# FFN1 of the last batch by seven half-width products per two tiles of d_ff, and batches 2 to 7 written out operation by operation

## The chip, the cores and the metric

The kernel runs on one core of one Trainium2 chip. The metric is the device time of one execution in microseconds, lower is better. Beside the times there is a profile of one execution: every instruction with its engine, start, duration and what it waited for. The engines are TensorE (PE, with its weight loads listed apart as PEld), VectorE (DVE), ScalarE (ACT), GpSimd (POOL, here an issuer of loads) and SyncE (SP, here an issuer of stores and transposes).

## The reference

Eight batches, twelve heads, 448 tokens, 64 values per head: attention with a squared ReLU in place of a softmax, then a feed-forward pair with a leaky ReLU whose slope differs by column.

```python
batch, n_heads, seq, head_dim = (8, 12, 448, 64)
scores = scale * np.matmul(q, k.transpose(0, 1, 3, 2))
attn = np.maximum(scores, 0.0) ** 2 / S
attn_out = np.matmul(attn, v)
x = attn_out.transpose(0, 2, 1, 3).reshape(B * S, H * D)        # 3584 x 768
h = x @ w_in                                                    # 768 x 2048
g = np.maximum(h, 0.0) + alpha * np.minimum(h, 0.0)
out = g @ w_out                                                 # 2048 x 768
```

## The kernel before, in words

**Attention.** Four heads of a batch form a quad; a batch has 3 quads, and there are 24. A quad's scores come in 7 chunks. A chunk (`c` in the plan) is four 64x64 matmuls of 448 columns into two PSUM banks (`score_mm`, L209). One ReLU empties both banks, on ACT (L218) or on DVE (L220), and a square follows in SBUF (`s`; DVE L231 or ACT L229). When the 7 squares of a quad are there, `v` runs 28 matmuls of 64x64 (L241) and two copies write the quad's part of `xT` (L253 on ACT, L255 on DVE). q and k reach the layout T through a copy into `perm` (L195) and a transposing DMA on SP's queue (L197); POOL touches the tile that landed (L418) and then issues the next loads.

**FFN1.** For each batch `xT` holds 6 slices of 128 by 448. A tile of d_ff (`f`, 16 per batch) is 6 full-array matmuls of 448 columns into one bank (L275). ACT makes `neg` = relu(-h) from the bank (L281), and DVE writes g = h + (1 - alpha) * neg as bf16 into `gT` (L282, one SCALAR_TENSOR_TENSOR). `gT` holds two batches: batch b may be written once every reader of batch b - 2 is through.

**FFN2.** Four tiles of 128 tokens are done plainly (`f2`, L300). The other 24 form 12 pairs. A pair is a 2x2 block product done in Winograd's form with 7 products of 8 matmuls each, 384 columns wide (L335), and not with 8 such products. Its sums S are made on DVE (L331), the sums of the weights `w_mix` once (L313), and the results are combined by ACT copies (L351, L356) and DVE additions (L340).

**Order.** The program is scheduled by hand. A plan is a string of words, and each word issues one or several instructions in that order on their engines; every engine takes its own in order and waits on semaphores for the others. Words of before are compound: `f` is the 6 matmuls, the ReLU and the DVE operation, `cADA` is three chunks with their ReLUs. One plan serves batches 3, 4 and 6 alike (`EACH`), the others have their own. PSUM has 8 banks; a word takes the bank that was taken longest ago (`one`, `take_pair`), so the words' order fixes the banks too. Batch 7 (`LAST`) runs its 16 `f`, then the last two FFN2 pairs. Its last product is cut in two (`p4e`, 256 and 128 columns), and its stores go alternately through SP and ACT from the word `z` on.

Of the kernel before, what the change touches and what calls it, by code (L numbers as in the profile page):

```python
# [20 lines left out]
def kernel(  # L21
# [50 lines left out]
    paired, two_queues = [], []  # L72
# [161 lines left out]
    def attnv(n, eng="AD"):  # L234
        ps = take_pair()
        vv = vraw.pop(n)
        for j in range(NJ):
            a = att.pop((n, j))
            for r in range(2):
                for s in range(2):  # L240
# [7 lines left out]
        if eng == "A":
            nc.scalar.activation(xT[b][:, g], ps[:, :, :S], ACTF.Copy, scale=out_scale)
            return  # L250
        for r in range(2):
            if eng[r] == "A":
                nc.scalar.activation(xT[b][:, g, r], ps[:, r, :S], ACTF.Copy, scale=out_scale)  # L253
            else:
                nc.vector.tensor_scalar(xT[b][:, g, r], ps[:, r, :S], out_scale, None, ALU.mult)  # L255
# [15 lines left out]
    gT = singles.tile([128, KF, 2 * S], BF16, name="gT")  # L271

    def f1_mm(ps, b, ff, ks):
        for km in ks:
            nc.tensor.matmul(ps, w_in_sb[:, km // 2, km % 2, bass.ts(ff, 128)],  # L275
# [3 lines left out]
    def f1_out(ps, b, ff):  # L279
        neg = neg_pool.tile([128, S], F32, tag="neg", name="neg")  # L280
        nc.scalar.activation(neg, ps, ACTF.Relu, scale=-1.0)  # L281
# [11 lines left out]
    def f2(sb, c, h, parts=None):  # L293

        first_col, width = COLS[h][0], COLS[h][1] - COLS[h][0]
        o = o_pool.tile([128, d_model - CUT], F32, tag="o", name="osb")
        for lo, hi in parts or ((0, width),):
            ps = take_bank()[:, :hi - lo]
            for ff in range(KF):
                nc.tensor.matmul(ps, gT[:, ff, bass.ts(c, 128)], w_out_sb[:, ff, first_col + lo:first_col + hi],  # L300
                                 start=(ff == 0), stop=(ff == KF - 1))
            nc.scalar.copy(o[:, lo:hi], ps)
            store(sb, c, first_col + lo, first_col + hi, o[:, lo:hi])
# [11 lines left out]
    class Pair:  # L315

        def __init__(self, a, b):
            self.a, self.b = a, b
            ga, gb = gT[:, :, bass.ts(a[1], 128)], gT[:, :, bass.ts(b[1], 128)]
            self.a11, self.a12, self.a21, self.a22 = ga[:, :KH], ga[:, KH:], gb[:, :KH], gb[:, KH:]  # L320
            self.s = {}

        def mix(self, *which):
            for i in which:
                t = self.s[2] if i == 4 else S_pool.tile([128, KH, 128], BF16, tag="S", name="S")
# [7 lines left out]
        def mm(self, ps, left, right, start):  # L333
            for i in range(KH):
                nc.tensor.matmul(ps, left[:, i], right[:, i], start=(start and i == 0), stop=(i == KH - 1),  # L335
                                 skip_group_check=not start)

        def plus(self, ps, u, keep=None):
            t = keep if keep is not None else o_pool.tile([128, d_model - CUT], F32, tag="o", name="osb")[:, :u.shape[-1]]
            nc.vector.tensor_tensor(t, ps, u, ALU.add)  # L340
            return t

        def kept(self, tag="u"):
            return u_pool.tile([128, NH], F32, tag=tag, name=tag)

        def p1(self):
            self.xb = hold()
            self.x = psum[:, self.xb, :NH]
            self.mm(self.x, self.a11, w_out_sb[:, :KH, :NH], True)
            self.m1 = self.kept("m")  # L350
            nc.scalar.copy(self.m1, self.x)  # L351

        def p2(self):
            self.mm(self.x, self.a12, w_out_sb[:, KH:, :NH], False)
            t = o_pool.tile([128, d_model - CUT], F32, tag="o", name="osb")[:, :NH]
            nc.scalar.copy(t, self.x)  # L356
            take(self.xb, 1)
            store(*self.a, 0, NH, t)
# [193 lines left out]
```

## Time and profile before

| | us |
|---|---|
| median of 3 runs | 373.29 (373.25, 373.29, 375.82) |
| span of the profiled execution, first to last instruction | 371.3 |
| TensorE with a matmul in it | 363.6 (98%) |
| VectorE busy | 278.0 (75%) |
| ScalarE busy | 274.7 (74%) |
| GpSimd busy | 71.7 (19%) |
| first matmul of batch 2's FFN1 | 109.18 |
| last matmul ends | 367.57 |

The page gives the span of the profiled execution and no time of its own beside it; the median of the runs lies 2.0 us above that span. Matmuls overlap in the array, so a matmul's recorded duration is longer than the distance to the next one; what a stream costs is the distance between starts. DVE and ACT records overlap in the same way by about a tenth of a microsecond. The granted TensorE clock is 1.00 in every stretch of the span.

### The profile page before, as it was taken

The numbers are of one execution on the slowest core, as the hardware profiler recorded it, in microseconds if no ns is written. First come the engines' busy times: TensorE is split into PE (matmuls) and PEld (weight loads), VectorE is DVE, ScalarE is ACT, GpSimd is POOL, SyncE is SP. The second block draws the span as 40 slices with busy tenths as digits, with TensorE's granted clock in tenths as the row PEclk, the third lists the DMA queues.
The fourth block names the chain that finished last, engine by engine and source line by source line (L and its number), as shares of the span: only waits on it lengthen the run. The fifth ranks groups of instructions, "written<-read, shape, count | busy, mean of one in ns | idle before, by whom it ended". The sixth has DMA issues, their size and how long they took to land.

```text
span 371.3 us, 7894 instructions
## 1 busy us (share of the span) xinstructions
PE 363.6 (98%) x3105; PEld 197.5 (53%) x3105; DVE 278.0 (75%) x445; ACT 274.7 (74%) x406; POOL 71.7 (19%) x120
## 2 busy tenths in 40 slices
PE   8799999999999999999999999999999999999995
PEld 6454564444554565545555455554555455555563
DVE  3989988885968989566887768888749667856653
ACT  5998676877997678885997859967699866964400
POOL 8566150304211222022020220202200000000000
PEclk9999999999999999999999999999999999999999
DMA  9999989999999868455882659727646201220024
GB/s 143 188 203 202 199 135 191 153 160 167 180 171 150 123 96 163 92 89 90 160 144 64 99 80 168 144 56 121 111 89 134 49 2 43 65 65 0 0 64 108
DMA packets 73557, 43.29 MB, mean 117 GB/s; under 512 B 40368, under 2 KB 73008, under 8 KB 73520
## 3 DMA queue, kind: packets, MB, share of 16 engines
q0 software_dynamic: 27136, 22.58, 42.0%
q1 hardware_dynamic: 45712, 19.61, 25.9%
q10 hardware_dynamic: 672, 0.59, 0.5%
q8 instruction: 24, 0.39, 0.4%
q14 instruction: 13, 0.11, 0.1%
HBM read 45.62 MB, written 11.01 MB: 153 GB/s over the span
## 4 chain that ended last, share of the span: by engine, by line
PE 94%; DVE 2%; ACT 2%; issue 1%; ACTq 0%
PE psum L275 38%; PE psum L335 30%; PE psum L241 9%; PE psum L209 9%; PE psum L300 6%; PE psum L183 1%; PE psum L165 1%; DVE gT L282 1%; ACT rl L218 1%; ACT xT L253 1%; ACT neg L281 1%; DVE w_mix L195 1%; DVE T L186 0%; DVE at L231 0%; DVE osb L340 0%
## 5 line engine op out<-in xcount | busy, mean ns | idle before, releaser
L275 PE MATMUL psum<-xT,w_in_sb 128*128 128x448 bf16 x768 | 150.4, 353 | 0.2 <-DVE gT L282 0.2
L282 DVE SCALAR_TENSOR_TENSOR gT<-neg,beta_sb,psum 128x448 bf16<-128x448 f32 x128 | 85.3, 679 | 43.4 <-ACT neg L281 42.1
L218 ACT ACTIVATE rl<-psum 128x896 bf16<-128x896 f32 x128 | 111.2, 925 | 6.7 <-PE psum L209 4.7
L275 PEld LDWEIGHTS <-w_in_sb 128*128 128x128 bf16 x768 | 73.4, 98 | 73.0 <-issue 6.8
L281 ACT ACTIVATE neg<-psum 128x448 f32<-128x448 f32 x128 | 68.5, 547 | 41.0 <-PE psum L275 32.7
L231 DVE TENSOR_TENSOR at<-rl 128x896 bf16<-128x896 bf16 x105 | 62.2, 620 | 0.5 <-ACT rl L218 0.2
L229 ACT ACTIVATE at<-rl 128x896 bf16<-128x896 bf16 x63 | 58.6, 952 | 0.3
L335 PEld LDWEIGHTS <-S 128*128 128x128 bf16 x384 | 36.7, 98 | 28.4 <-issue 5.3
L335 PE MATMUL psum<-w_mix,S 128*128 128x384 bf16 x288 | 49.8, 326 | 0.2
L220 DVE TENSOR_SCALAR rl<-psum 128x896 bf16<-128x896 f32 x40 | 43.2, 1086 | 8.7 <-PE psum L209 8.1
L209 PE MATMUL psum<-T 64*64 64x448 bf16 x672 | 45.9, 357 | 2.0 <-DVE T L186 1.0
L418 POOL COPY landed<-T 1x1 bf16<-1x1 bf16 x18 | 3.3, 181 | 206.1 <-DMA T<-perm 182.9
L335 PEld LDWEIGHTS <-gT 128*128 128x128 bf16 x296 | 28.3, 98 | 20.2 <-issue 1.8
L241 PE MATMUL psum<-at,vraw 64*64 64x448 bf16 x672 | 36.6, 350 | 0.0
L335 PE MATMUL psum<-w_out_sb,gT 128*128 128x384 bf16 x192 | 34.0, 326 | 0.0
L340 DVE TENSOR_TENSOR osb<-psum,u 128x384 f32<-128x384 f32 (+2 forms) x37 | 20.2, 547 | 12.6 <-PE psum L335 8.2
L209 PEld LDWEIGHTS <-T 64*64 64x64 bf16 x672 | 17.4, 105 | 22.7 <-issue 14.8
L241 PEld LDWEIGHTS <-vraw 64*64 64x64 bf16 x672 | 21.2, 106 | 11.9 <-issue 2.9
L300 PE MATMUL psum<-w_out_sb,gT 128*128 128x256 bf16 (+1 forms) x128 | 22.0, 326 | 0.1
L255 DVE TENSOR_SCALAR xT<-psum 128x448 bf16<-128x448 f32 x24 | 14.9, 622 | 8.9 <-PE psum L241 8.3
L253 ACT ACTIVATE xT<-psum 128x448 bf16<-128x448 f32 x24 | 13.3, 556 | 9.1 <-PE psum L241 8.7
L356 ACT COPY osb<-psum 128x384 f32<-128x384 f32 x12 | 5.8, 480 | 17.4 <-PE psum L335 17.4
(45 smaller groups left out, 242.0 us busy)
## 6 DMA issues: line engine op xcount, KB each, us to landing
out_dram<-osb SPq DMA_DIRECT2D x91, 96.0 KB, 2.2
vraw<-in_v_dram POOLq DMA_DIRECT2D x24, 224.0 KB, 6.5
qraw<-in_q_dram POOLq DMA_DIRECT2D x23, 224.0 KB, 4.1
kraw<-in_k_dram POOLq DMA_DIRECT2D x23, 224.0 KB, 5.3
w_in_sb<-in_moe_w_in_dram POOLq DMA_DIRECT2D x16, 192.0 KB, 8.0
w_out_sb<-in_moe_w_out_dram POOLq DMA_DIRECT2D x4, 512.0 KB, 9.5
w_out_sb<-in_moe_w_out_dram POOLq DMA_DIRECT2D x4, 256.0 KB, 8.8
out_dram<-osb SPq DMA_DIRECT2D x8, 128.0 KB, 3.2
```

The lines of the kernel that those rows point to most:

```text
L209: nc.tensor.matmul(ps[64 * c:64 * c + 64, r, :S], t[64 * r:64 * r + 64, 1, j, 64 * c:64 * c + 64], t[64 * r:64 * r + 64, 0, :, 64 * c:64 * ...
L218: nc.scalar.activation(rl, ps[:, :, :S], ACTF.Relu)
L220: nc.vector.tensor_scalar(rl, ps[:, :, :S], 0.0, None, ALU.max)
L229: nc.scalar.activation(a, rl, ACTF.Square)
L231: nc.vector.tensor_tensor(a, rl, rl, ALU.mult)
L241: nc.tensor.matmul(ps[64 * s:64 * s + 64, r, :S], vv[64 * r:64 * r + 64, s, j, :], a[64 * r:64 * r + 64, s], start=(j == 0), stop=(j == NJ ...
L275: nc.tensor.matmul(ps, w_in_sb[:, km // 2, km % 2, bass.ts(ff, 128)], xT[b][:, km // 2, km % 2, :], start=(km == 0), stop=(km == KM - 1))
L281: nc.scalar.activation(neg, ps, ACTF.Relu, scale=-1.0)
L282: nc.vector.scalar_tensor_tensor(gT[:, ff, (b % 2) * S:(b % 2) * S + S], neg, beta_sb[:, ff:ff + 1], ps, ALU.mult, ALU.add)
L300: nc.tensor.matmul(ps, gT[:, ff, bass.ts(c, 128)], w_out_sb[:, ff, first_col + lo:first_col + hi], start=(ff == 0), stop=(ff == KF - 1))
L335: nc.tensor.matmul(ps, left[:, i], right[:, i], start=(start and i == 0), stop=(i == KH - 1), skip_group_check=not start)
L340: nc.vector.tensor_tensor(t, ps, u, ALU.add)
```

## The change

Up to and including batch 1 the instructions are the same. Behind that two things differ.

**FFN1 of batch 7.** Its 16 tiles of d_ff are taken two at a time, in 8 `Quad`s. Two tiles of d_ff by 448 tokens by 768 is a 2x2 block product: weights in four quarters of 3 x 128 by 128, tokens in four quarters of 3 x 128 by 224. It is done by 7 products of 3 matmuls with 224 columns, in place of 2 x 6 matmuls with 448 columns (the same work as 8 products). The sums of the weights (`W`, `w_in_mix`) and of the tokens (`T`, `tok_mix`) are made on DVE; they lie in buffers of the raw, v, perm and at pools, and the third weight sum replaces a quarter of `w_in_sb`. A quad owns two PSUM banks, x and y. Its products run in the order 1, 2/5, 6, 7, 3, 4 with steps between them on ACT (small letters s, u, w) or DVE (capitals): s copies 224 columns from bank x to bank y, u and w copy 224 columns from y to SBUF, v and z add 224 columns (DVE, from PSUM and SBUF into PSUM). n is one ACT ReLU over both banks (896 columns), g and h are the two SCALAR_TENSOR_TENSOR that write `gT`.

**Order of batches 2 to 7.** One plan of 965 words replaces the six. A word is now one operation with its bank written out: `f6` the 6 matmuls into bank 6, `N6` the ReLU, `G6` the DVE operation, `c4` a chunk's matmuls into banks 4 and 5, `r4A` its ReLU on ACT, `+b63` product 6 of pair b into bank 3, `-b6` its output, `*ba` a sum. So operations of several words are interleaved as the string says, and more chunks stand early: 63 chunks by the word `+e42` against 50 up to the same amount of TensorE work before. `p4e` is gone; `z` stands two words before the last product.

```diff
-        if not paired:
-            return order[0]
-        mate = max(free, key=lambda i: taken[i]) ^ 1
-        return mate if mate in order[:4] and taken[mate] < 10**9 else order[0]
+        return free[0]
...
+    def w_in_mix(i, p, count, home):
+        a11, a12, a21, a22 = w_in_quarters(p, count)
...
+        x, y, op = {1: (a21, a22, ALU.add), 2: (made(1), a11, ALU.subtract),
+                    3: (a11, a21, ALU.subtract), 4: (a12, made(2), ALU.subtract)}[i]
+        nc.vector.tensor_tensor(t, x, y, op)
...
+    def tok_mix(i):
...
+        x, y, op = {1: (b12, b11, ALU.subtract), 2: (b22, tok_sum.get(1), ALU.subtract),
+                    3: (b22, b12, ALU.subtract), 4: (b21, tok_sum.get(2), ALU.subtract)}[i]
+        nc.vector.tensor_tensor(t, x, y, op)
...
+        def mm(self, ps, left, right, start):
+            for k in range(KI):
+                nc.tensor.matmul(ps, left[:, k], right[:, k], start=(start and k == 0), stop=(k == KI - 1),
+                                 skip_group_check=not start)
...
+            if c == "1":
+                self.mm(x[:, :HS], a11, b11, True)
+            elif c == "2":
+                self.mm(x[:, :HS], a12, b21, False)
+            elif c == "3":
+                self.mm(x[:, HS:S], self.w(4), b22, False)
+            elif c == "4":
+                self.mm(y[:, :HS], a22, tok_sum[4], False)
+            elif c == "5":
+                self.mm(x[:, HS:S], self.w(1), tok_sum[1], False)
+            elif c == "6":
+                self.mm(y[:, :HS], self.w(2), tok_sum[2], False)
+            elif c == "7":
+                self.mm(y[:, :HS], self.w(3), tok_sum[3], False)
+            elif c in "sS":
+                (nc.scalar.copy if c == "s" else nc.vector.tensor_copy)(y[:, :HS], x[:, :HS])
+            elif c in "uU":
+                (nc.scalar.copy if c == "u" else nc.vector.tensor_copy)(u[:, :HS], y[:, :HS])
+            elif c in "wW":
+                (nc.scalar.copy if c == "w" else nc.vector.tensor_copy)(u[:, HS:], y[:, :HS])
+            elif c == "v":
+                nc.vector.tensor_tensor(y[:, HS:S], x[:, HS:S], u[:, HS:], ALU.add)
+            elif c == "z":
+                nc.vector.tensor_tensor(x[:, HS:S], x[:, HS:S], u[:, :HS], ALU.add)
+            elif c == "n":
...
+                nc.scalar.activation(self.neg, psum[:, self.lo:self.lo + 2, :S], ACTF.Relu, scale=-1.0)
+            elif c in "gh":
...
+                nc.vector.scalar_tensor_tensor(gT[:, ff, (NB % 2) * S:(NB % 2) * S + S], self.neg[:, i],
+                                               beta_sb[:, ff:ff + 1], psum[:, self.lo + i, :S], ALU.mult, ALU.add)
...
-    LAST = """B f s0A f f f f s3A s2A s2A f f s2A f f f f f f pc f f s0A f p1 r1 pa pb p2 p6 p7 pd ra p5 rb rc p4 p3 r6 z r7 rd r5 r2 r3 r4e"""
...
+    P[4] = """*ba f0 f1 sA kqD kkA *bb f2 sD sA N0 +b63 N2 sD sD *bc f4 G0 N1 G2 N4 -b6 f5 c6 c2 G1 c0 G4 sA f4 r6D N5 f6 sD t r2A kqD r0A f7 N4 c2 kkA G5 G4 N6 r2A
```

The rows below show what stands on two engines at the places that the prediction speaks of. First VectorE at the start of batch 2, before; gT rows are FFN1's operations, at rows squares, rl rows ReLUs, S rows the sums of an FFN2 pair.

```order
97 L220 TENSOR_SCALAR rl<-psum 128x896
98 L282 SCALAR_TENSOR_TENSOR gT<-neg,beta_sb,psum 128x448 x2
99 L231 TENSOR_TENSOR at<-rl 128x896 x3
100 L282 SCALAR_TENSOR_TENSOR gT<-neg,beta_sb,psum 128x448 x2
101 L231 TENSOR_TENSOR at<-rl 128x896
102 L282 SCALAR_TENSOR_TENSOR gT<-neg,beta_sb,psum 128x448 x4
```

VectorE at the same place after the change:

```order
97 L217 TENSOR_SCALAR rl<-psum 128x896
98 L415 TENSOR_TENSOR S<-gT 128x1024
99 L693 COPY perm<-qraw 128x896
100 L415 TENSOR_TENSOR S<-S,gT 128x1024
101 L228 TENSOR_TENSOR at<-rl 128x896 x3
102 L415 TENSOR_TENSOR S<-gT 128x1024
103 L659 SCALAR_TENSOR_TENSOR gT<-neg,beta_sb,psum 128x448 x2
104 L396 TENSOR_TENSOR u<-psum,m 128x384
105 L659 SCALAR_TENSOR_TENSOR gT<-neg,beta_sb,psum 128x448 x2
106 L217 TENSOR_SCALAR rl<-psum 128x896
```

The sums of the second FFN2 pair, one copy into `perm` and a pair's output have moved ahead of batch 2's first FFN1 operations, which now stand behind seven other operations and not behind one.

Second, VectorE in FFN1 of batch 7 and behind it, before:

```order
279 L282 SCALAR_TENSOR_TENSOR gT<-neg,beta_sb,psum 128x448 x13
280 L331 TENSOR_TENSOR S<-gT 128x1024
281 L282 SCALAR_TENSOR_TENSOR gT<-neg,beta_sb,psum 128x448 x3
282 L331 TENSOR_TENSOR S<-gT 128x1024
283 L331 TENSOR_TENSOR S<-S,gT 128x1024
```

VectorE in a piece of FFN1 of batch 7 after the change; L525, L527 and L529 are s, u and w of a quad, L531 is v, L533 is z, L541 is g or h, L464 a sum of weights, L415 and L396 belong to FFN2 pairs:

```order
330 L533 TENSOR_TENSOR psum<-psum,uu 128x224
331 L396 TENSOR_TENSOR osb<-psum,u 128x384
332 L464 TENSOR_TENSOR w_in_sb<-w_in_sb 128x3x2x128
333 L533 TENSOR_TENSOR psum<-psum,uu 128x224
334 L541 SCALAR_TENSOR_TENSOR gT<-ng,beta_sb,psum 128x448
335 L525 COPY psum<-psum 128x224
336 L541 SCALAR_TENSOR_TENSOR gT<-ng,beta_sb,psum 128x448 x2
337 L415 TENSOR_TENSOR S<-S,gT 128x1024
338 L464 TENSOR_TENSOR w_in_sb<-w_in_sb 128x3x2x128
339 L525 COPY psum<-psum 128x224
340 L541 SCALAR_TENSOR_TENSOR gT<-ng,beta_sb,psum 128x448
```

Thirteen like operations in a row are replaced by operations of two or three quads in turn, with two FFN2 pairs (i and j of the plan) between them; before, those pairs stood ahead of batch 7's FFN1.

More of the change, by code (lines that the diff above doesn't have):

```diff
@@ L71 @@
     taken = [0] * 8
-    paired, two_queues = [], []
+    two_queues = []
     clock = [0]
@@ L189, in turn_dma @@
         if n in (5, 7, 8):
+            assert not mixed[2 + n % 2]
             w = w_mix[2 + n % 2].rearrange("p k c -> p (k c)")[:, :4 * NJ * D]
@@ L291, in store, with f2_mm, f2_out, f2 @@
             eng.dma_start(out=rows[j][:, lo:hi], in_=t[64 * u:64 * u + 64])
-    def f2(sb, c, h, parts=None):
-        first_col, width = COLS[h][0], COLS[h][1] - COLS[h][0]
-        o = o_pool.tile([128, d_model - CUT], F32, tag="o", name="osb")
[L297 to L303, printed above, removed]
+    def f2_mm(sb, c, h, i):
+        may_read((sb, c))
+        if (sb, c) in f2_half:
+            f2_done.add((sb, c))
+            has_read((sb, c))
+        f2_half.add((sb, c))
+        lo, hi = COLS[h]
+        for ff in range(KF):
+            nc.tensor.matmul(psum[:, i, :hi - lo], gT[:, ff, bass.ts(c, 128)], w_out_sb[:, ff, lo:hi],
+                             start=(ff == 0), stop=(ff == KF - 1))
+    def f2_out(sb, c, h, i):
+        lo, hi = COLS[h]
+        o = o_pool.tile([128, d_model - CUT], F32, tag="o", name="osb")
+        nc.scalar.copy(o[:, :hi - lo], psum[:, i, :hi - lo])
+        store(sb, c, lo, hi, o[:, :hi - lo])
+    def f2(sb, c, h):
+        i = one()
+        take(i, 1)
+        f2_mm(sb, c, h, i)
+        f2_out(sb, c, h, i)
+    mixed = [0] * 4
     def weight_mix(i, lo, hi):
+        assert not i or mixed[{1: 0, 2: 0, 3: 1}[i]] > mixed[i]
+        mixed[i] += 1
         b11, b12 = w_out_sb[:, lo:hi, :NH], w_out_sb[:, lo:hi, NH:]
@@ L331, in mix @@
                 nc.vector.tensor_tensor(t, x, y, op)
[L333 to L358, printed above, removed]
@@ L392, in p4y, with run @@
-        def p4y(self):
-            self.p4x(256, NH)
-        def p4e(self):
-            self.p4(((0, 256), (256, NH)))
-        def p3(self):
-            self.mm(self.z, self.s[4], w_out_sb[:, KH:, NH:], False)
-            store(*self.a, NH, d_model, self.plus(self.z, self.u2))
-            take(self.zb, 1)
+        def run(self, name):
+            if name in "23":
+                i = self.held.pop({"2": "1", "3": "5"}[name])
+                take(i, 1)
+            elif name in "15":
+                i = self.held[name] = hold()
+            else:
+                i = one()
+                take(i, 1)
+            self.product(name, psum[:, i, :NH])
+            self.output(name)
@@ new lines @@
+Q44 Q5u Q3h Q614 Q4z Q4n -j5 Q6S Q52 Q4g Q57 Q55 Q5w Q4h Q5v Q66 +j36 Q712 Q53 Q6u Q7S Q5z -j3 Q67 Q54 Q76 Q6w Q7U Q62 Q65 Q72 Q5n Q6v Q77 Q75 Q63 Q7w
+Q7v Q6z Q64 Q73 Q5g Q74 +j47 Q6n Q7z Q7n Q5h +k16 -k1A Q6g Q7g Q6h Q7h +l10 *lc +k26 +l71 *ka *kb *kc +k64 +k75 +k42 -l1D *kd *la -j4 -k6 *lb -k2A
++k53 +l64 -k7 -k5 -k4 +k33 *ld +l55 +l42 -k3 -l6 -l7 -l5 +l35 -l4 z -l3 +l20 -l2A"""
+    for i in range(4):
+        walk(P[i])
+    Line(walk)(P[4])
+    assert all(p.done == 7 for p in walk.pairs)
+    assert not stream and not late and turn["v"] == NQ and f2_done == {(0, 0), (0, 1), (0, 2), (2, 5)}
```

331 lines of the change are left out of this document (257 added, 74 removed).

## The prediction

> **What bounds the kernel now.** I read the page first: the share of each engine, and the chain that ended last.
>
> ```profile
> PE 363.6 (98%) x3105; PEld 197.5 (53%) x3105; DVE 278.0 (75%) x445; ACT 274.7 (74%) x406; POOL 71.7 (19%) x120
> PE 94%; DVE 2%; ACT 2%; issue 1%; ACTq 0%
> ```
>
> The chain is TensorE's. A busy 98% alone would not say so, because matmuls overlap. So I take the distance between starts from the timeline, at three widths: FFN1 (448 columns, the window opens after its first matmul), FFN2 products (384), and the last seven matmuls of the program (128). The fourth row is the weight loads of those narrow ones.
>
> ```profile
> 331.22 18.13 PE L275 MATMUL psum<-xT,w_in_sb 128*128 128x448 bf16 x95
> 349.19 4.06 PE L335 MATMUL psum<-w_out_sb,gT 128*128 128x384 bf16 x24
> 353.09 1.14 PE L335 MATMUL psum<-w_mix,S 128*128 128x384 bf16 x6
> 367.02 0.55 PE L335 MATMUL psum<-w_mix,gT 128*128 128x128 bf16 x7
> L335 PEld LDWEIGHTS <-gT 128*128 128x128 bf16 x8 | 0.5, 98 | 0.0
> L335 PE MATMUL psum<-w_mix,gT 128*128 128x128 bf16 x8 | 0.6, 219 | 0.0
> ```
>
> 95 matmuls of 448 columns take 349.19 - 331.22 = 17.97 us, 189.2 ns each. 24 of 384 take 353.09 - 349.19 = 3.90 us, 162.5 ns. Seven of 128 take 0.55 us; less the 0.219 of the last, six distances of 55 ns. The three lie on a line: 0.417 ns per column and 2.4 ns. So in FFN1 of batch 7 TensorE streams without a gap, and a change gains only by fewer columns or by waits elsewhere.
>
> How much waiting is there elsewhere? The chain gives a whole batch between two equal places:
>
> ```profile
> 152.57 9.19 PE psum L275 x48
> 198.52 9.19 PE psum L275 x48
> ```
>
> 45.95 us. It holds 96 matmuls of 448 (18.17 us), 14 products of 8 by 162.5 ns (18.20), 21 chunks and 3 words `v`, whose 64x64 matmuls run four at a time: 42 groups of one 448-column stream, 0.188 (7.90): 44.27 in all. The other 1.68 are turns between full-array and 64x64 matmuls, and waits. A turn is priced by this:
>
> ```profile
> 104.81 0.33 PE L335 MATMUL psum<-w_mix,gT 128*128 128x384 bf16 x1
> 105.06 0.76 PE L209 MATMUL psum<-T 64*64 64x448 bf16 x12
> 105.76 1.47 PE L335 MATMUL psum<-w_out_sb,S 128*128 128x384 bf16 x8
> 188.22 0.76 PE L209 MATMUL psum<-T 64*64 64x448 bf16 x12
> 189.04 2.27 PE L335 MATMUL psum<-w_mix,S 128*128 128x384 bf16 x13
> ```
>
> Three chunks (0.564) take 0.70 at 105.06, so 0.14 to turn back. The full-array matmul at 104.81 streams until 104.97, and the chunk starts at 105.06, 0.09 later: about 0.22 for a pair of turns. At 188.22 the same work takes 0.82: there TensorE waits 0.12. With 6 pairs of turns the batch has 1.32, and 0.36 of waits is left, of which about 0.25 are such visible ones. Over batches 2 to 6 that is 5 x 0.25, some **1.2 us that a better order can win**, and no more.
>
> **The change part by part.** The order of the built program gives the counts. FFN1 of batch 7: 96 matmuls of 448 go, 8 x 7 x 3 = 168 of 224 come. On the line, 224 columns cost 0.417 x 224 + 2.4 = 95.8 ns. 96 x 0.1892 = 18.16 against 168 x 0.0958 = 16.10: **-2.07 us**, on the path.
>
> The weight loads are the question here: 98 ns each, more than 95.8. But the 128-column matmuls above have a load each of 98 ns and follow at 55 ns, so loads overlap and do not set the pace. The Trainium skill says otherwise on its page TensorE: Matmul & The Clock Gate, section Back-to-back issue gap: with a weight load per matmul it gives about 81 ns for 128 columns, and under LDWEIGHTS columns / 1.2, which is 107 ns for 128. At 107 ns the 168 would take 18.0 us, an estimate by that page, and the sum below would end 1.9 us later. The row of 55 ns speaks against both figures, so I count nothing for it.
>
> Turns: the order has 34 stretches of 64x64 matmuls from batch 2 on, 28 before. 6 x 0.22 = **+1.3 us**, on the path.
>
> The old waits of 1.2 us go, where the new order covers them. What new ones come depends on DVE and ACT:
>
> ```profile
> 109.20:225.80 116.60, 116.48 (x927) 62.22 (x924) 88.53 (x142) 91.72 (x138) 21.68 (x37) 1.00 0.69 115
> 331.00:371.30 40.30, 36.57 (x220) 20.80 (x216) 21.97 (x36) 11.16 (x21) 0.00 (x0) 1.00 0.18 46
> 112.97 1.69 DVE L231 TENSOR_TENSOR at<-rl 128x896 bf16<-128x896 bf16 x3
> 114.58 1.27 DVE L282 SCALAR_TENSOR_TENSOR gT<-neg,beta_sb,psum 128x448 bf16<-128x448 f32 x2
> L282 DVE SCALAR_TENSOR_TENSOR gT<-neg,beta_sb,psum 128x448 bf16<-128x448 f32 x48 | 32.0, 679 | 19.5 <-ACT neg L281 19.3
> L220 DVE TENSOR_SCALAR rl<-psum 128x896 bf16<-128x896 f32 x40 | 43.2, 1086 | 8.7 <-PE psum L209 8.1 <-issue 0.4
> L331 DVE TENSOR_TENSOR S<-gT 128x1024 bf16<-128x1024 bf16 x24 | 15.9, 685 | 0.0
> L313 DVE TENSOR_TENSOR w_mix<-w_out_sb 128x1536 bf16<-128x1536 bf16 x4 | 3.7, 952 | 0.0
> L229 ACT ACTIVATE at<-rl 128x896 bf16<-128x896 bf16 x63 | 58.6, 952 | 0.3
> L253 ACT ACTIVATE xT<-psum 128x448 bf16<-128x448 f32 x24 | 13.3, 556 | 9.1 <-PE psum L241 8.7
> ```
>
> In a row of windows the numbers behind the stretch are its length, then PE, PEld, DVE, ACT. Back to back an operation costs 0.09 less than its record: three squares 1.69 = 2 x 0.535 + 0.62, two gT operations 1.27 = 0.59 + 0.68. The first 469 words of the new order hold, by the spacings above, as much TensorE work as the stretch 109.2 to 225.8. In them DVE has 11 more ReLUs (1.00 each), 11 squares (0.53) and 7 copies into perm (about 0.53, as a square of the same shape), less 2 sums, 2 outputs and an xT copy (2.7): 88.5 + 11.0 + 5.8 + 3.7 - 2.7 = **106.3 of 116.6**, 91%. ACT gains 6 squares (0.95), 5 xT copies (0.56) and 2 ReLUs and loses a perm copy and 4 outputs: about +7, 99 of 116.6. So both still fit, with 10 us of slack on DVE.
>
> I followed the order by hand with these costs, a matmul's result 0.2 after its stream. At the start of batch 2 the two engines stand at
>
> ```profile
> 109.18 7.17 PE L275 MATMUL psum<-xT,w_in_sb 128*128 128x448 bf16 x37
> 109.56 1.08 DVE L220 TENSOR_SCALAR rl<-psum 128x896 bf16<-128x896 f32 x1
> ```
>
> From 109.56 DVE has a ReLU, three sums, a copy, three squares, gT of banks 0 and 2, an output and gT of bank 1: 1.0 + 1.8 + 0.53 + 1.6 + 1.2 + 0.47 + 0.6 = 7.2, done at 116.8. TensorE by then has f0, f1, f2 (3.41), b63 (1.30), f4, f5 (2.27), two chunks and a turn (0.47) from 109.18, so it is at 116.63 and c0, which needs bank 1, waits 0.25. The next f4 waits as much for G4. From the start of batch 3's FFN1 I followed 60 us and found no wait: the banks come free 0.3 to 3 us early. In the last 75 us I found one of 0.14 (product 3 of the last quad, behind v). So 0.65 in 155 of 258 us; scaled to the whole **+1.1 us**.
>
> In the Quad part DVE has 16 additions (v, z), 8 copies, 4 token sums and 15 weight sums more. No row has an operation that writes PSUM from DVE or ACT. The nearest are reads of it:
>
> ```profile
> L340 DVE TENSOR_TENSOR osb<-psum,u 128x256 f32<-128x256 f32 x1 | 0.4, 425 | 0.3 <-PE psum L335 0.3
> L340 DVE TENSOR_TENSOR osb<-psum,u 128x128 f32<-128x128 f32 x1 | 0.3, 291 | 0.0
> L302 ACT COPY osb<-psum 128x256 f32<-128x256 f32 x4 | 1.5, 373 | 3.7 <-PE psum L300 3.7
> ```
>
> 224 columns on that line: 0.39 on DVE, and under 0.37 on ACT. The bounds are 0.29 (128 columns) and 0.68 (the gT operation on 448); I take 0.39, nearest in width. 24 x 0.30 back to back = 7.2 us; weight sums of 768 elements 0.55 (between 685 ns for 1024 and 952 for 1536, 0.52 per element), 14 x 0.46 + 0.87 = 7.3; token sums 4 x 0.42 = 1.7. Together 16 us, spread over the last 100 us, in which DVE had room (21.97 of 40.30 at the end): hidden, but for 10 us in the middle of the quads, where with these costs the order has 9.7 us of DVE to 10.1 of TensorE. If that cover goes, each 0.1 us per operation there costs about 1 us. ACT has spare time there. What hides a quad's chain of some 6.5 us (product, copy, product, copy ... ReLU, two gT operations) is the other quads and 14 FFN2 products of 1.30.
>
> The end: the last product is whole, so its copy on ACT reads 384 columns.
>
> ```profile
> 367.61 0.29 DVE osb L340
> L356 ACT COPY osb<-psum 128x384 f32<-128x384 f32 x12 | 5.8, 480 | 17.4 <-PE psum L335 17.4
> out_dram<-osb ACTq DMA_DIRECT2D x3, 96.0 KB, 2.4
> out_dram<-osb ACTq DMA_DIRECT2D x1, 32.0 KB, 1.9
> ```
>
> Copy +0.19, landing +0.5, less some 0.5 because the stores of the piece before no longer stand in the queues: **+0.1** (0 to 0.7).
>
> ```profile
> T<-perm SPq DMA_TRANSPOSE x16, 4.0
> ```
>
> Moved DMAs: the transposes and loads follow the perm copies. Each quad's copies stand at least 7 us of TensorE work ahead of its first chunk, against the 4.0 us from transpose to landing; the stores on SP's queue have no reader. Nothing counted.
>
> Sum: -2.07 + 1.3 - 1.2 + 1.1 + 0.1 = -0.8; span 371.3 - 0.8 = 370.5, and with the 2.0 us between span and the median of the runs **372.5 us**.
>
> **The rivals.** (1) The new waits do not come: -2.07 + 1.3 - 1.2 + 0.1 = -1.9, 371.4 us. For it: the stretch of 60 us without one. Against: the 0.25 above.
>
> (2) Operations that write PSUM cost more, 0.2 us each (towards the row of 448 columns). In the Quad part the cover on DVE is gone, 8 quads wait in turn for v and z: 16 x 0.2 = 3.2, of which I let 0.7 be hidden; 372.5 + 2.5 = 375.0 us. Nothing in the profile excludes it.
>
> (3) Slower: DVE becomes the bound from batch 2 to 4. Before, it stood idle 19.5 us ahead of its 48 gT operations in that stretch, waiting for ACT (row above). The new order leaves it 10.3. If it idles as before, 106.3 + 19.5 = 125.8 against 116.6, 9.2 us more than TensorE needs: 382 us. It decides from 10 us of such idling. Against it: other work of DVE now stands between the gT operations, so that the wait for ACT passes under it.
>
> **How the numbers follow.** Forecast 0.50, rival 1 0.20, rival 2 0.16, rival 3 0.14. What a measurement here can tell from no change is about 1%, 3.7 us. To gain that much, TensorE would have to save more than -2.07 and all waits together, 3.3 us without the turns: 0.03 for faster. Slower by over 1%, beyond 377.0: rival 3, 0.14. Same 0.83. The range runs from 371.0 (rival 1 with turns at 0.15) to 376.5 (rival 2 with 0.1 more an operation, or rival 3 with 14 us idle).
>
> **What would show it.** In the new profile: 224-column matmuls about 96 ns apart (the Quad line's 18 or so in the windows); 64x64 stretches 34; DVE busy near 106 in the first 117 us behind 109.2, and its idle time ahead of gT operations under 10; a v or z row near 0.39. Rival 2 would show as PE waiting for DVE L531 or L533, rival 3 as PE waiting for DVE's gT and rl operations in batches 2 to 4. I am wrong if the loads set the pace of the narrow matmuls, or if TensorE waits over 3 us in all from batch 2 on.

## The result, and the profile after

The changed kernel takes 379.23 us (median of 7 runs, 375.17 to 382.76), the kernel before 373.25 us (7 runs, 372.88 to 375.82). The ratio is 1.0121 with a 95% interval of 1.0085 to 1.0158: slower by somewhat over 1%. It leaves out the two runs of 381.04 and 382.76 us, which lie over 1.5% above the fastest run of the same kernel, and so is smaller than the quotient of the two medians, 1.016. The forecast was 372.5 us with a range up to 376.5, so it missed, and it missed on the side to which it had given 0.14. The runs of the changed kernel also spread over 7.6 us, those of the kernel before over 2.9.

The profiled execution took 379.88 us, its span 378.1. From its page, the busy time and shares of the engines, three rows of the 40 slices, and the chain that ended last, by engine and by line:

```profile
PE 363.5 (96%) x3166; PEld 202.0 (53%) x3169; DVE 303.2 (80%) x502; ACT 264.3 (70%) x399; POOL 72.3 (19%) x120
PE   8699999999999599999999999999999999999995
PEclk9999999999999699999999999999999999999999
DMA  9999989999999787978999853824123120021125
PE 85%; DMA 7%; DVE 4%; ACT 2%; issue 1%; POOL 1%; ACTq 0%; DVEq 0%; POOLq 0%; SPq 0%
PE psum L303 30%; PE psum L379 27%; PE psum L237 9%; PE psum L206 8%; PE psum L330 6%; DMA T<-perm 5%; PE psum L501 4%; DMA kraw<-in_k_dram 2%; DVE gT L311 1%; PE psum L175 1%; ACT neg L310 1%; DVE w_mix L188 1%; DVE rl L217 0%; DVE at L228 0%; ACT perm L188 0%
```

TensorE is as busy as before in sum (363.5 against 363.6 us) and the span is 6.8 us longer. The loss is in one place: the fourteenth of the 40 slices, about 123 to 132 us, shows TensorE at 5 tenths and its clock at 6. And a new name stands in the chain, `DMA T<-perm` with 5%: the DMA that transposes a quad's q and k out of the buffer `perm`.

The timeline of TensorE there (start, length, line, operation), and then the waits of all engines in 118 to 128 us (in all, times, longest):

```profile
121.51 0.57 PE L206 MATMUL psum<-T 64*64 64x448 bf16 x8
126.97 2.83 PE L237 MATMUL psum<-at,vraw 64*64 64x448 bf16 x28 [4.89 <-DVE gT L659]
```

```profile
POOL landed L435 <- DMA T<-perm: 11.4, 1, 11.4
DVE perm L693 <- DMA T<-perm: 5.5, 1, 5.5
PEld L237 <- issue: 5.1, 1, 5.1
PE psum L237 <- DVE gT L659: 4.9, 1, 4.9
ACT perm L693 <- DMA T<-perm: 4.8, 1, 4.8
```

TensorE has nothing to do for about 5 us, ahead of the product of scores and v that the plan calls v4 (word 49 of the plan, counted from 0). It waits for DVE's operation into gT, which frees banks 4 and 5. But DVE is not busy then: it stands for 5.5 us in front of a copy into `perm`, ACT for 4.8 us in front of another, and both wait for the transposing DMA. These are the copies of quad 12 (words 36 `kqD` and 41 `kkA`), which stand ahead of G5 and G4 in the queues, and `perm` has one buffer, which quad 11's DMA is still reading. The chain of waits, in order of time (start, length):

```profile
111.80 0.53 DVE perm L693
112.33 0.18 DVE S L415
112.50 12.52 DMA T<-perm
...
125.12 0.62 DVE perm L693
125.74 1.19 DVE gT L659 x2
...
126.97 2.83 PE psum L237 x28
```

Issued at 112.50, the transposition landed at 125.03, 12.5 us later, where the typical one before took 4.0. But 4.0 is a median of 16. In the kernel before the three transpositions issued at 102.5, 114.0 and 123.6 us took 6.8 to 7.0 us, and that of quad 11 is the second of them. The rows below show it, first before and then after. GpSimd issues four loads at this place, the last two in the `vraw` rows. Before, the transposition goes out 1.9 us behind the last of them, at 114.03; in the changed kernel it goes out between the two, at 112.50. The `landed` row is GpSimd's one-element copy right behind a landing.

```profile
111.40 1.44 POOL L124 DMA_DIRECT2D vraw<-in_v_dram  x2
114.03 12.73 SPq L197 DMA_TRANSPOSE T<-perm  x2
121.17 0.18 POOL L418 COPY landed<-T 1x1 bf16<-1x1 bf16 x1 [8.33 <-DMA T<-perm]
112.35 1.43 POOL L116 DMA_DIRECT2D vraw<-in_v_dram  x2
112.50 27.61 SPq L193 DMA_TRANSPOSE T<-perm  x3
125.15 0.18 POOL L435 COPY landed<-T 1x1 bf16<-1x1 bf16 x1 [11.37 <-DMA T<-perm]
```

Then the clock: windows of 6 us give, in the column behind POOL (0.90, 0.53, 1.00), the granted clock of TensorE.

```profile
120.00:126.00 6.00, 2.08 (x17) 0.84 (x16) 0.88 (x2) 1.17 (x2) 0.52 (x2) 0.90 0.75 87
126.00:132.00 6.00, 5.03 (x39) 2.39 (x39) 5.26 (x8) 4.00 (x7) 1.80 (x3) 0.53 0.97 148
132.00:138.00 6.00, 6.00 (x41) 2.90 (x40) 4.11 (x6) 4.31 (x9) 2.32 (x4) 1.00 0.67 98
```

After the wait the matmuls run at about half speed until 131.5 us. By the distances between matmul starts the wait cost 5.06 us. The slow stretch cost 2.2: the same matmuls, from v4 on, take that much less in the run after_again (below), where the clock stays at 1.00 there. From 132 us on TensorE's starts show nothing more than 0.23 us late. 378.1 less these 7.3 is 370.8, half a us under the span before.

One more difference between the two kernels shows in the times at which transpositions are issued. In the kernel before, quads 11 and 18 were issued at 114.0 and 215.8 us, 14.5 us apart per quad; in the changed kernel at 112.5 and 190.6, 11.2 us apart. The new order asks for the same transpositions and loads in less time. The loads of q, k and v that GpSimd issues behind a landing take 6.5 to 8.5 us from the first issue to the last landing. In the kernel before (from 140 to 190 us) the next transposition goes out when they have landed, or 0.1 us earlier; in the changed kernel it goes out 3 to 7 us before the last of them has landed. What the transpositions took from issue to landing in 130 to 220 us, first before and then (130 to 200 us) after:

```profile
DMA to landing us min/median/max: 4.0/4.0/4.3
```

```profile
DMA to landing us min/median/max: 5.0/6.1/7.9
```

### The profile page after: what moved, and what is told of

Its sections match the earlier page's. It is cut to its first block, busy times and chain, and to the rows that moved or that the text cites. A ratio compares the mean times of both kernels' runs of the same rounds, so it can differ in the third digit from the quotient of the medians.

```text
span 378.1 us, 8029 instructions
## 1 busy us (share of the span) xinstructions
PE 363.5 (96%) x3166; PEld 202.0 (53%) x3169; DVE 303.2 (80%) x502; ACT 264.3 (70%) x399; POOL 72.3 (19%) x120
## 4 chain that ended last, share of the span: by engine, by line
PE 85%; DMA 7%; DVE 4%; ACT 2%; issue 1%; POOL 1%; ACTq 0%; DVEq 0%; POOLq 0%; SPq 0%
PE psum L303 30%; PE psum L379 27%; PE psum L237 9%; PE psum L206 8%; PE psum L330 6%; DMA T<-perm 5%; PE psum L501 4%; DMA kraw<-in_k_dram 2%; DVE gT L311 1%; PE psum L175 1%; ACT neg L310 1%; DVE w_mix L188 1%; DVE rl L217 0%; DVE at L228 0%; ACT perm L188 0%
## 5 line engine op out<-in xcount | busy, mean ns | idle before, releaser
L303 PE MATMUL psum<-xT,w_in_sb 128*128 128x448 bf16 x672 | 134.4, 354 | 0.5 <-ACT xT L249 0.3
L215 ACT ACTIVATE rl<-psum 128x896 bf16<-128x896 f32 x118 | 104.7, 924 | 13.8 <-PE psum L206 13.5
L303 PEld LDWEIGHTS <-w_in_sb 128*128 128x128 bf16 x672 | 63.9, 98 | 66.1 <-issue 10.1
L217 DVE TENSOR_SCALAR rl<-psum 128x896 bf16<-128x896 f32 x50 | 54.2, 1087 | 17.5 <-PE psum L206 17.1
L653 ACT ACTIVATE neg<-psum 128x448 f32<-128x448 f32 x80 | 43.0, 548 | 28.3 <-PE psum L303 16.8
L659 DVE SCALAR_TENSOR_TENSOR gT<-neg,beta_sb,psum 128x448 bf16<-128x448 f32 x80 | 52.6, 676 | 9.2 <-ACT neg L653 8.2
L379 PE MATMUL psum<-w_mix,S 128*128 128x384 bf16 x288 | 51.5, 326 | 0.0
L206 PE MATMUL psum<-T 64*64 64x448 bf16 x672 | 47.0, 358 | 1.4 <-ACT rl L215 1.0
L396 DVE TENSOR_TENSOR osb<-psum,u 128x384 f32<-128x384 f32 x36 | 19.8, 553 | 15.3 <-PE psum L379 11.1
L311 DVE SCALAR_TENSOR_TENSOR gT<-neg,beta_sb,psum 128x448 bf16<-128x448 f32 x32 | 21.0, 678 | 3.9 <-ACT neg L310 3.3
L310 ACT ACTIVATE neg<-psum 128x448 f32<-128x448 f32 x32 | 17.2, 548 | 8.8 <-PE psum L303 6.1
L249 ACT ACTIVATE xT<-psum 128x448 bf16<-128x448 f32 x30 | 16.5, 552 | 6.2 <-PE psum L237 6.1
```

The source lines that it names most:

```text
L206: nc.tensor.matmul(ps[64 * c:64 * c + 64, r, :S], t[64 * r:64 * r + 64, 1, j, 64 * c:64 * c + 64], t[64 * r:64 * r + 64, 0, :, 64 * c:64 * ...
L215: nc.scalar.activation(rl, ps[:, :, :S], ACTF.Relu)
L217: nc.vector.tensor_scalar(rl, ps[:, :, :S], 0.0, None, ALU.max)
L311: nc.vector.scalar_tensor_tensor(gT[:, ff, (b % 2) * S:(b % 2) * S + S], neg, beta_sb[:, ff:ff + 1], ps, ALU.mult, ALU.add)
L659: nc.vector.scalar_tensor_tensor(gT[:, ff, (b % 2) * S:(b % 2) * S + S], neg, beta_sb[:, ff:ff + 1], ps, ALU.mult, ALU.add)
```

## The experiments

My theory after the trace (A): the two copies stand too early in the queues for a transposition that lands late, everything behind them waits, and the idle TensorE loses its clock. The rival (B) was the prediction's own: VectorE and ScalarE simply have too much to do in batches 2 to 4, and `perm` is only where it shows.

### late_copies: quad 12's and 13's copies moved back

```
- f6 sD t r2A kqD r0A f7 N4 c2 kkA G5 G4 N6 r2A
+ f6 sD t r2A r0A f7 N4 c2 G5 G4 N6 r2A
...
- sA sA N6 G6 t f0 f1 N0 x41A sD f7 N1 G1 f6
+ sA sA N6 G6 f0 f1 N0 x41A kkA sD kqD f7 N1 G1 t f6
```

Quad 13's two copies moved some 14 and 9 words back in the same way.

> The plan of batches 2 to 7 with quad 12's two copies into perm moved from words 36 and 41 to behind the squares that follow x41A (behind v4, word 49), their t behind them, and quad 13's two copies some 14 and 9 words later; all else as in the changed kernel, and nothing left out. Theory A (the 5.06 us wait of TensorE at 121.73 is DVE's and ACT's queues standing behind these two copies, which wait for quad 11's transposing DMA to give the one perm buffer back, and the 2 us after it are matmuls at half the clock because of that wait): the wait and the slow stretch go, span 378.1 - 5.1 - 2.0 = 371.0, time 372.3 to 373.3, with no gap of TensorE over 0.5 us between 110 and 140 us. Theory B (VectorE and ScalarE have too much to do in batches 2 to 4, the old rival, and perm is only where it shows): the waits come back elsewhere, time 376 to 380.

Measured: 380.26 us (5 runs), ratio 1.0173 (1.0133 to 1.0213). The wait at 121 us is gone, but the time isn't. The chain of late_copies from 143 us on:

```profile
143.48 0.62 DVE perm L693
...
144.23 10.75 DMA T<-perm
...
155.07 0.62 DVE perm L693
155.69 0.60 DVE S L415
156.29 0.54 DVE at L228
156.82 0.60 DVE gT L659
...
159.41 5.25 PE psum L303 x18
```

The same thing has happened three quads later: quad 14's transposition of 10.75 us, quad 15's copy that stands waiting for its end, and DVE's gT operations behind the copy. TensorE waited 1.84 us at 143 and 1.35, 1.17 and 0.30 from 156 on, and then ran 3 us at half speed. Theory A in its narrow form (one badly placed pair of words) fell, and the time was just above the 376 to 380 that B said.

### second_home: another buffer for quad 12 alone, no word moved

```
-                self.perm = perm_pool.tile([128, 2, NJ, 2, D], BF16, tag="perm", name="perm")
+                self.perm = (T_pool.tile([128, 2, NJ, 2, D], BF16, tag="T", name="perm2") if self.quad == 12 else
+                             perm_pool.tile([128, 2, NJ, 2, D], BF16, tag="perm", name="perm"))
```

> The changed kernel in its own order, every word in its place; only quad 12's copies write to a fourth buffer of T's pool, which is free then, not to perm. Nothing left out. Theory A: the copies at words 36 and 41 find their buffer free, DVE and ACT go on to the words that free banks 4 and 5, the wait of 5.06 us and the slow stretch go without any word being moved: 372.3 to 373.5, though quad 11's transposition may still take 12 us. Theory B (too much work on VectorE and ScalarE): 376 to 380. A third (the transposition's lateness itself is what TensorE waits for, by the chunks that read T): the wait stays, some us later, 375 to 378.

Measured: 374.17 us (12 runs, 371.81 to 380.47), ratio 1.0015 (0.9986 to 1.0043), 0.7 over the upper end of what theory A said. The order of the work on every engine is that of the changed kernel and its amount too, and 5 us have gone; so B, which needs the amount of work, is out. Quad 11's transposition took longer than in the changed kernel (14.5 us, landing at 127.44), and TensorE no longer stood at 121 us. Waits of 0.3 to 0.9 us were left at 134 to 136 and 156 to 158 us. Only the buffer differs, so the hand-over of the single `perm` is the cause of the wait at 121 us.

### later_loads: two of the loads beside quad 11's transposition issued later

```
- l10 cA cA s3A +a6 Lq12 Lv10 +ad Lv11 +a7
+ l10 cA cA s3A +a6 Lq12 +ad +a7
...
             land(n)
+            for late_v in (10, 11) if n == 11 else ():
+                load_v(late_v)
```

> The changed kernel in its own order, only the loads of v for quads 10 and 11, which GpSimd issued at 112.35 to 113.78 beside quad 11's transposing DMA (issued 112.50, landed 125.03), are issued behind that quad's landing. Nothing left out. Theory A with loads as the cause of the late landing: the transposition beside two loads, not four, lands after 6 to 9 us, not 12.5, the wait shrinks from 5.06 us to 0 to 1.5 us, time 372.5 to 374.5. If the transposition is late for another reason (the stores of out beside it, or itself): it still lands after 11 to 13 us, and the time stays at 377 to 380.

Measured: 377.87 us (6 runs), ratio 1.0124 (1.0078 to 1.0170). GpSimd's one-element copy behind each transposition shows when it landed:

```profile
108.26 0.18 POOL L435 COPY landed<-T 1x1 bf16<-1x1 bf16 x1 [6.28 <-DMA T<-perm]
117.82 0.18 POOL L435 COPY landed<-T 1x1 bf16<-1x1 bf16 x1 [7.62 <-DMA T<-perm]
132.62 0.18 POOL L435 COPY landed<-T 1x1 bf16<-1x1 bf16 x1 [10.70 <-DMA T<-perm]
```

Quad 11's transposition, issued at 111.7, now landed after 6.0 us, and TensorE did not wait at 121. So the loads made it late. But the two loads now stood beside quad 12's, which was issued at 120.3 and took 12.2 us; quad 13's copies waited 2.6 and 4.4 us for it, and TensorE 2.2 and 1.4 us at 132 to 137, with half speed behind. The expected time failed, because the loads were only moved from one transposition to the next.

### no_v_loads: a third of the loads left out

```
     def load_v(n):
+        if n >= 12:
+            vraw[n] = vraw[11] if 11 in vraw else v_kept[0]
+            v_kept.append(vraw[n])
+            return
```

> The changed kernel in its own order, with the loads of v of quads 12 to 23 left out (their products read quad 11's v, so the output is another one): a third of the bytes that GpSimd's loads move beside the transpositions. Theory A2 with the loads as the cause of the late landings: quad 11's transposition still has four loads less one beside it (landing 8 to 11 us, a wait of 1 to 4 us left at 121 us), those of quads 13 to 18 land after 4 to 7 us, time 373 to 377. If loads are not the cause: landings as in the changed kernel (7 to 12 us), time 377 to 380.

Measured: 377.79 us (6 runs, 375.59 to 378.82; ratio 1.0102, 1.0067 to 1.0137), just outside the 373 to 377 expected. The profile shows what the loads do:

```profile
DMA to landing us min/median/max: 4.0/4.4/5.0
```

From 130 to 200 us the transpositions landed after 4.4 us instead of 6.1, close to the 4.0 before, and TensorE had no wait there. Quad 11's, which still had the same four loads beside it, took 10.2 us, and 2.72 us of wait stayed at 121, again with half speed behind it. So loads beside it make a transposition late. The Trainium skill says as much in general (DMA: Bandwidth & Descriptors, section Issuing engines are not separate DMA queues): transfers started by different engines run on the same 16 DMA engines and interleave there. The 4.4 and 6.1 us agree with it. How much of it is their number and how much the moment at which they are issued, no run separates.

That gave the second form of the theory (A2): the new plan hands `perm` on every 10 to 11 us; its cycle is a copy, a transposition that takes 4 us alone and 5 to 12.5 beside loads, and the next copy; the loads of quad n+2 start when quad n has landed and so run into the next transposition. Where a copy comes up before the landing, all that stands behind it in DVE's and ACT's queues waits.

### spaced: all copies of quads 12 to 21 set apart

The two copies and the `t` of each of these quads were taken out and put back by TensorE's work since batch 2's start: 17.8, 29.8, 41.1, 52.0, 62.8, 74.1, 86.3, 99.4, 110.4 and 121.5 us. They had been at 10 to 11, 19 to 22, 28 to 32, 42, 49 to 51, 60 to 63, 71 to 74, 84 to 85, 93 to 94 and 105 to 109, so that they moved by 6 to 18 us, and each quad's first scores still come 13 to 20 us behind its new place (all worked out by the prediction's spacings).

The edit at quad 12, as one of ten:

```
- t r2A kqD r0A f7 N4 c2 kkA G5 G4 N6
+ t r2A r0A f7 N4 c2 G5 G4 N6
...
- sA sA N6 G6 t f0 f1 N0 x41A sD f7 N1 G1
+ sA sA N6 G6 f0 f1 N0 x41A sD f7 kqD kkA t N1 G1
```

> The changed kernel with the two copies of each of quads 12 to 21 and their t moved to 10 to 13 us of TensorE's work apart (17.8, 29.8, 41.1, 52.0, 62.8, 74.1, 86.3, 99.4, 110.4, 121.5 us after batch 2's start), so that each stands behind the landing of the transposition before it even where that takes 11 us, and still lands ahead of its quad's first scores; all other words as they were, nothing left out. Theory A2 (the new plan hands perm on every 10 us, the transposing DMA beside loads keeps it for 7 to 12 us, and what stands behind the copies in DVE's and ACT's queues makes TensorE wait; late_copies only moved the place of the wait): no wait over 0.5 us between 110 and 350 us, 379.88 - 7.87 (all that the gaps of over 0.13 us cost in the changed kernel's trace) = 372.0, so 371.3 to 372.8. Theory B (VectorE and ScalarE are too full in batches 2 to 4): 375 or more.

Measured: 374.39 us (12 runs, 373.76 to 375.32), ratio 1.0026 (1.0007 to 1.0046). No copy waited for a DMA that TensorE then waited for; 5 us of the changed kernel's loss are back, and its spread is 1.6 us. It is 1.6 over the upper end of what I expected (372.8), and the trace shows where most of that is: two new waits of TensorE, 0.54 us at 224.6 and 0.98 at 234.3 us, right behind the copies of quads 20 and 21.

### spaced_undone: the seven products taken back

```
-            elif c == "3":
-                self.mm(x[:, HS:S], self.w(4), b22, False)
...
+            if c in "1274":
+                ps, ff, lo = {"1": (x, 0, 0), "2": (x, 0, KI), "7": (y, 1, 0), "4": (y, 1, KI)}[c]
+                f1_mm(ps[:, :S], NB, 2 * p + ff, range(lo, lo + KI))
```

All words that begin with W or T (sums of w_in and xT) are left out of the plan, and s, u, w, v, z of a quad issue nothing, nor do its products 3, 5 and 6.

> As spaced, with batch 7's FFN1 by 12 products of 448 tokens per two tiles of d_ff at the places of the seven products' words, and without the sums of w_in, of xT and of the parts in PSUM. Theory A2: the prediction's 2.07 us, nothing of it hidden or lost: 2.07 slower than spaced, 373.3 to 374.9. Rival (what the products save is given back by the copies and sums that they need): within 0.5 us of spaced.

Measured: 376.16 us (6 runs), ratio 1.0083 (1.0053 to 1.0113), so 1.77 us above spaced in the medians; the spans of the two profiles are 372.1 and 374.3, 2.2 apart. The prediction's -2.07 for the products is between them, so the sums eat little of it, if anything.

**quads_undone** was the same edit on late_copies.

> As late_copies, but batch 7's FFN1 by 12 products of 448 tokens per two tiles at the places of the seven products (8 products of halves, not 7), without the sums of w_in, of xT and of the parts in PSUM; relu and PReLU of each pair of tiles stay where they are. Theory A (the seven products save what the prediction summed, 2.07 us, and the sums are all hidden): 2.07 us slower than late_copies, so 374.4 to 375.4. Rival (the sums on VectorE and the copies on ScalarE cost at the end of the program what the products save): within 0.7 us of late_copies, or faster.

Measured: 381.77 us (6 runs, 378.71 to 385.98), 1.5 above late_copies, whose runs had 379.11 to 381.16. With waits of several us that come and go in both, this tells nothing about 2 us; spaced_undone took its place.

### busy_wait and busy_wait64: TensorE kept busy in the wait

```
+        def do_y(self, w):
+            for _ in range(int(w)):
+                nc.tensor.matmul(psum[:, 6, 256:384], idle, idle, start=True, stop=True)
...
- G6 N7 c0 v4 x40A
+ G6 N7 c0 y60 v4 x40A
```

> The changed kernel with 60 matmuls of a constant tile (128 columns, 3.3 us in all) put ahead of v4 (word 49), where TensorE waited 5.06 us; they write to columns of a bank that nothing reads. If the slow matmuls from 127 to 131.5 us come from TensorE's idle time: the wait keeps its end, the clock of the 24 matmuls behind it stays at 1.00, and the time is some 2 us under the changed kernel's, 376 to 378. If they come from something else: half speed behind the wait as before, 379 to 380.

Measured: 382.00 us (4 runs). A failed experiment: bank 6 still had a reader, so the 60 matmuls waited themselves (5.78 us) and then ran at half speed, 5.85 us for 60 of 128 columns. In busy_wait64 they write to 64 columns of bank 0 that nobody else touches.

```
-                nc.tensor.matmul(psum[:, 6, 256:384], idle, idle, start=True, stop=True)
+                nc.tensor.matmul(psum[:, 0, S:], idle, idle[:, :512 - S], start=True, stop=True)
...
- G6 N7 c0 y60 v4 x40A
+ G6 N7 c0 y100 v4 x40A
```

> busy_wait again, since its 60 matmuls stood themselves behind the wait (their bank was still being read) and ran at half speed: now 100 matmuls of 64 columns, into 64 columns of a bank that nothing else writes or reads, so that they wait for nothing and lie inside the wait. If the slow matmuls behind the wait come from TensorE's idle time: the wait of v4 ends where it did, and the matmuls behind it run at the full clock (PEclk 1.00 in 120 to 136 us); some 2 us under the changed kernel in its own run of this call. If the clock falls for another reason: half speed for some 4.5 us behind the wait, as there.

> The changed kernel as it is, on the chip of these runs: 377 to 381, one wait of 3 to 6 us at 121 us, and half speed for some 4.5 us behind it.

Measured: 377.98 us (4 runs, 374.84 to 380.96) for busy_wait64, 379.22 (4 runs, 376.57 to 380.74) for after_again; 1.2 us apart, less than either spreads. The traces say more. busy_wait64 at the place of the wait, TensorE's timeline and then two windows:

```profile
121.56 3.09 PE L726 MATMUL psum<-idle 128*128 128x64 bf16 x100
125.70 1.52 PE L237 MATMUL psum<-at,vraw 64*64 64x448 bf16 x28 [1.05 <-DVE gT L659]
```

```profile
120.00:126.00 6.00, 4.95 (x122) 3.86 (x124) 2.07 (x4) 1.79 (x3) 1.78 (x4) 1.00 0.54 65
126.00:132.00 6.00, 6.00 (x57) 3.22 (x49) 5.66 (x9) 5.04 (x9) 0.55 (x1) 1.00 1.19 155
```

v4 started no earlier than the banks allowed (125.70), but it took 1.52 us, not 2.83, and the clock stayed at 1.00. In after_again the wait at 121 was 2.50 us, not the 3 to 6 expected, and no slow stretch followed; three waits close together from 155.9 on (1.53, 1.17, 0.30) were followed by one. So it is the idle time that costs the clock. Over all traces of this study, single waits up to 2.50 us left it alone, and single waits of 2.72 us and more, and pairs and threes that came to 2.8 and more within 5 us, were followed by 2.8 to 5.7 us at half speed. The Trainium skill (TensorE: Matmul & The Clock Gate, section Why this matters for your kernels) warns of idle gaps over some 3 us; the traces agree, with the bound here a little lower.

### spaced2 and spaced3: the last waits

spaced2 puts one copy of quad 20 and one of quad 21 on each engine, and quad 21's 2 us earlier.

```
- r2D v4 kqD kkD t sA x40A
+ r2D v4 kqD kkA t sA x40A
...
- *fb v2 c4 x20A r4A sD c6 *ga +f20 kqA kkA t x21A
+ *fb v2 kqD kkA t c4 x20A r4A sD c6 *ga +f20 x21A
```

> As spaced, with quad 20's and quad 21's copies one on VectorE and one on ScalarE each (they were two on VectorE, two on ScalarE), quad 21's 2 us earlier: in the trace of spaced the two waits of TensorE over 0.4 us, at 224.6 (0.54 over its pitch) and 234.3 us (0.35 and 0.62), stand right behind these copies. If the copies' place in one queue is what made them: both go, 1.5 us less than spaced, 372.3 to 373.5, so within 0.2% of the kernel before, and what is left is the prediction's sum (-0.8 us). If they come from the density of work there: waits of the same size elsewhere, 374 to 375.

Measured: 373.28 us (12 runs, 372.46 to 374.97), ratio 1.0006 (0.9991 to 1.0021): 1.1 us under spaced, and equal to the kernel before. Of the two waits that were to go, the one at 234.3 us went; the one at 224.6 shrank from 0.54 to 0.44. The idle times of TensorE that the view of waits lists from 109 us to its end:

```profile
PE psum L303 <- DVE gT L659: 0.3, 1, 0.3
PE psum L303 <- ACT xT L249: 0.3, 1, 0.3
PE psum L206 <- ACT rl L215: 0.2, 1, 0.2
```

spaced3 gives quad 12 the buffer of second_home as well, and puts quad 20's second copy 4 us later on VectorE.

```
- v4 kqD kkA t sA x40A c6 c2 -e6 sA r6A sD sD +e71 x41D *ed -e7 *fa +f10 -f1A r2A sD c4
+ v4 kqD sA x40A c6 c2 -e6 sA r6A sD sD +e71 x41D *ed -e7 *fa +f10 -f1A r2A sD kkD t c4
```

> As spaced2, with quad 12's copies in a fourth buffer of T's pool (as in second_home: quad 11's transposition had still landed only 0.6 us ahead of them), and quad 20's second copy on VectorE, 4 us later, where it had 0.86 us to spare (behind it stood the wait of 0.44 us at 224.6). Theory A2 (with the hand-over of perm out of the way what is left is the prediction's sum): 0.4 us and the spread of spaced2's runs less, 372.3 to 373.0, a ratio of 0.997 to 0.999 to the kernel before. If the new order costs in itself what the products save: as spaced2, 373.3, ratio 1.000 to 1.001.

Measured: 373.29 us (12 runs, 372.56 to 379.60), ratio 1.0014 (0.9995 to 1.0033): no gain, and the spread is back. The wait at 224.6 is gone, and others of 0.55, 0.43 and 0.53 us came at 184.5, 186.8 and 233.2 us. That is the second of the two outcomes that were expected: what is left of waits and of the end takes back what the products save. I found no version that beats the kernel before.

## Why the prediction was wrong, point by point

**The step that failed** is "Moved DMAs", with its "Nothing counted". It compared 4.0 us from issue to landing with the 7 us by which each quad's copies stand ahead of that quad's first scores, and so asked whether the scores would come too early. In the changed kernel's trace they hardly did: behind 100 us one weight load of TensorE waited 0.4 us for a transposition, and no matmul. The step did not ask when `perm` would be free for the next copies, nor what stands behind those copies on DVE and ACT, and it took 4.0 us for a price, though it is the price of a transposition with few loads beside it, and three of the 16 in its own trace had taken 7. The runs put in its place: 5 to 12.5 us beside loads (no_v_loads: 4.4 without a third of them), a hand-over every 11.2 us instead of 14.5, a wait of TensorE of 2.5 to 5 us for one copy that comes too early, and 2.2 us more from the clock, a term that the forecast did not have. Setting the copies apart (spaced, spaced2) took back 4.8 and 5.9 of the 6.0 us. One of the prediction's own signs of being wrong came true: TensorE waiting over 3 us in all.

**The other terms** can be read in spaced2, where that step is mended. Its last matmul ends at 366.89 us, that of the kernel before at 367.57: -0.68. The forecast for this part was -2.07 + 1.3 - 1.2 + 1.1 = -0.9.

- The products, -2.07: right. In the changed kernel's trace, the first and the twelfth of a row of groups of three matmuls:

```profile
350.05 0.45 PE L501 MATMUL psum<-xT,w_in_sb 128*128 128x224 bf16 x3
...
353.21 0.45 PE L501 MATMUL psum<-ts,w_in_sb 128*128 128x224 bf16 x3
```

From the one to the other, in 3.16 us, 33 matmuls start, 95.8 ns each, as forecast, though each has its own weight load. Over all 168 it is 96.8. The Trainium skill's 107 ns for a weight load (TensorE: Matmul & The Clock Gate, section LDWEIGHTS), by which it would have been 1.9 us more, does not set the pace here.

- Turns: 34 stretches of 64x64 matmuls, 28 before, as forecast. Their +1.3 and the -1.2 of the old waits were not measured alone; what is left for the two together, -0.68 less -2.07 and less the 1.5 of new waits, is -0.1, where +0.1 was forecast.
- New waits, 1.1: of the two at the start of batch 2 that of f4 came (0.20 us; 0.25 forecast); c0 found its bank free (the prediction's own times, 116.8 less 116.63, give 0.17 for it, not 0.25), and the first matmul of FFN1 waited 0.32 us, not forecast, for ScalarE's copy into xT. The one at product 3 of the last quad came (0.17; 0.14). By the distances between starts all of them come to 1.5 us in spaced2. Half of that is at 129.8 and 225.2 us, where the changed kernel has no such wait, so that 1.1 is near 1.5 in part by luck.
- The end, +0.1 (0 to 0.7): from the last matmul to the end of the span it is 3.72 us before, 4.18 in spaced2, so +0.46, inside the bounds and mis-sized.

Together spaced2's span is 371.1 against 371.3, so -0.2, where -0.8 was forecast; the median of its runs, 373.28, would lie in the prediction's range. The 12 runs lie between 372.46 and 374.97; what makes some of them 2 us longer stays open, since only one execution of each kernel has a trace.

**The rivals.** (2), dearer operations that write PSUM: out. The rows of v and z:

```profile
L533 DVE TENSOR_TENSOR psum<-psum,uu 128x224 f32<-128x224 f32 x8 | 3.1, 394 | 0.0
L531 DVE TENSOR_TENSOR psum<-psum,uu 128x224 f32<-128x224 f32 x8 | 3.1, 395 | 0.9 <-ACT uu L529 0.5 <-ACT ng L536 0.3 <-PE psum L501 0.2
```

0.39 us, the value taken. (3), DVE as the bound in batches 2 to 4, had the right stretch and the wrong reason. In spaced2 DVE's work there, the third of the busy times, and its idle time ahead of gT operations are:

```profile
109.52:226.10 116.58, 115.89 (x996) 59.46 (x996) 104.82 (x166) 96.96 (x144) 24.83 (x41) 1.00 0.85 125
L659 DVE SCALAR_TENSOR_TENSOR gT<-neg,beta_sb,psum 128x448 bf16<-128x448 f32 x48 | 31.4, 677 | 4.3 <-ACT neg L653 3.6
```

104.8 of 116.6 us (106.3 forecast) and 4.3 us of idling, where 10 would have been needed. DVE was full, but it was a queue that stood still, not a queue that was too long, that cost the time. (1), no new waits at all, was not met either. The 0.14 for slower stood on rival 3 alone; none of the three rivals was a wait on a single buffer.

## What to carry to other kernels

When a change moves operations that release or claim a single buffer, follow the buffer's cycle (copy, transfer, next copy) and compare its period with the transfer's time beside the traffic that the same change brings nearer. A median landing time from the old order is not that time: here it hid three of 7 us among the 4.0. An operation that may wait for a DMA belongs where the work behind it in its queue has time, not merely where its own result is wanted. And a wait of TensorE that exceeds some 2.5 us is to be priced with the slow matmuls behind it.

## What the runs showed of the hardware

A transposing DMA of 0.46 MB inside the core's memory took 4.0 us from issue to landing with little beside it (the kernel before, 130 to 220 us), a median of 4.4 with the loads of q and k alone beside it (no_v_loads), 5.0 to 7.9 with those of v as well (the changed kernel, 130 to 200 us), and 10.0 to 14.5 for quad 11's, which went out among four loads (the changed kernel, after_again, second_home and no_v_loads). TensorE ran 2.8 to 5.7 us at half speed after idling 2.7 us or more. 100 matmuls of 64 columns took 3.09 us, and the clock stayed at 1.00 behind them (busy_wait64). The trace of the kernel before had landings of 4.0 to 4.8 us and the three of 7, and the clock was 1.00 as long as matmuls ran.
